# Gated MLP: the last product as a closing stage over blocks of 1024 positions, from seven products of half blocks

## Chip, cores and metric

One core of a Trainium2 chip runs the whole program. The metric is the device time of one execution in microseconds (us), median of several runs. Differences under 0.2% (2 us here) are not told from no change.

## What is computed

Three stages follow one another on a batch of 8 sequences of 576 positions: attention over 32 memory slots, a gated mixing layer, and a gated MLP. The change concerns the last one:

```python
h = np.maximum(x @ w_in, 0.0)                  # [8, 576, 1024]
u, v = h[..., :512], h[..., 512:]
v_n = (v - mean(v)) / np.sqrt(var(v) + 1e-06)  # over the last axis
v_s = np.einsum('ts,bsd->btd', w_spatial, v_n) + b_spatial[None, :, None]
gated = u * v_s                                # [8, 576, 512]
return (gated @ w_out).astype(np.float32)      # w_out: [512, 512]
```

## The kernel before

Every product of this stage is made in three terms: each fp32 operand x is split into a rounded part h (an ACT copy to the type fp32r) and the remainder x - h (a DVE subtraction); `split` (L116) makes both. `three` (L104) lists the terms h·h, l·h, h·l, and `gemm` (L94) issues the matmuls, all recorded at L99.

The MLP stage goes over eight blocks b, one for each sequence. A block has 512 positions (two halves of `HALF` = 256); the 64 positions left over of all eight sequences form a ninth block, made ahead of the loop. For each block:

- `load_x2` (L601) fetches the block's input from DRAM and forms seven operands of its quarters (four subtractions on POOL, seven splits), as steps that are called between other work.
- `uv` (L875) makes the v half of h and then the u half, each from seven products of half blocks instead of eight. A `Group` (L837) holds four output quarters; `step(q)` makes product q into a PSUM bank of its own (6 matmuls of 256 columns) and adds it to the quarters that need it: two ACT copies, five DVE additions out of PSUM and two additions on POOL or DVE for each group. Two groups alternate, in the order 1, 6, 2, 7, 5, 3, 4. When a group of v is done, `layer_norm` (L824) and `finish` (L914) normalise its tiles t and split them into `vn_h`, `vn_l` (in the buffers W3h, W3l), while PE is on the u half.
- `spatial(b, hf)` makes v_s for 288 positions at a time: for each of four chunks c, 14 matmuls of 288 columns over the tiles t = 0 to 3 of v and the left-over positions; then DVE adds the bias, multiplies by u in PSUM (L986, L995), and a split out of PSUM gives the gated values gh, gl (buffers kh, kl).
- `project(b, hf)` (L1003) makes the last product: four chunks m, each of 12 matmuls of 288 columns against the weights wo (buffers W2h, W2l), an ACT copy (L1016) and a store.

Four of a block's eight output chunks follow its spatial product; the other four are kept as `left` and called as fillers inside the next block's v and u halves, two in each. So PE's stream is: v, u (with fillers), spatial, four chunks, and so on.

The program is written in this order, but the instructions of each engine are put in their final order by a scheduler when the program is built; each engine then runs its own in that order and waits on semaphores. All DMAs of this stage are issued from SP's queue, in order.

Of the kernel before, what the change touches and what calls it, by code (L numbers as in the profile page):

```python
# [8 lines left out]
F32 = mybir.dt.float32  # L9
# [18 lines left out]
HALF = 256  # L28
# [6 lines left out]
ORDER = "ICWWKMQDWLRWqrwwaaaawaabbababxxbbwbbxxWWww"  # L35

# [7 lines left out]
def kernel(  # L44
# [40 lines left out]
    x2r = dram.tile([128, KC, B, S - 2 * HALF], F32, name="x2r", tag="x2r")  # L85
    x2d = [dram.tile([128, KC, 2 * HALF], F32, name=f"x2d{b}", tag=f"x2d{b}") for b in range(B)]
# [8 lines left out]
    def gemm(out, pairs, part=0, parts=1):  # L95

        n = len(pairs)
        for i in range(part * n // parts, (part + 1) * n // parts):
            x = nc.tensor.matmul(  # L99
                out=out, lhsT=pairs[i][0], rhs=pairs[i][1], start=i == 0, stop=i == n - 1  # L100
            )
        return x
# [422 lines left out]
    def w_in_steps():  # L525
# [61 lines left out]
        wo.extend(pair("W2", [128, KC, DM]))  # L587
        for c in range(KC):
            split(wo_raw[:, c], wo[0][:, c], wo[1][:, c])
            yield  # L590
        parts_of("W1", wi_u)
        for q, a in ((0, a11), (4, s2), (1, a12), (5, a21), (3, s1), (6, s4), (2, a22)):
            split(a, wi_u[0][:, q], wi_u[1][:, q])
            yield
# [6 lines left out]
    def load_x2(n):  # L601
# [31 lines left out]
        ts = {}  # L633
# [7 lines left out]
        if rest:  # L641
# [19 lines left out]
            yield  # L661
            put(5, b12)
            yield
            put(3, b11)
            yield
        else:
            for x in ((b12, 0, 1), (b11, 0, 0), (b21, 1, 0), (b22, 1, 1)):
                fetch_x2(*x)
            yield
            put(0, b11)  # L670
# [15 lines left out]
            yield  # L686
            put(5, b12)
            yield
            put(3, b11)
            yield  # L690
        put(6, b21)
        x2s[n] = [ts[q] for q in range(7)]
# [116 lines left out]
    def w_s_steps(places, todo):  # L809

        raw = {}
        for n, (hf, t) in enumerate(todo):
            raw[hf, t] = places[n // 3][:, n % 3 * HB:(n % 3 + 1) * HB].bitcast(F32)
            nc.sync.dma_start(out=raw[hf, t], in_=w_sT[t * 128:(t + 1) * 128, hf * HB:(hf + 1) * HB])
        yield
        for (hf, t), x in raw.items():
            ws[t, hf] = pieces.pop(0), pieces.pop(0)
            split(x, *ws[t, hf])
            yield
# [17 lines left out]
    class Group:  # L837
# [3 lines left out]
        def __init__(self, at, out, done, engine=nc.gpsimd):  # L841
            self.at, self.out, self.done, self.engine = at, out, done, engine

        def step(self, q):
            c11, c12, c21, c22 = self.out
            acc = bank(next(mm))[:, 0:HALF]
            a, b = self.at(q)
            gemm(acc, three(*a, *b))

            def add(engine, dst, x, y):  # L850
                engine.tensor_tensor(out=dst, in0=x, in1=y, op=ALU.add)  # L851

            if q == 1:
                copied[0] = nc.scalar.activation(out=c11, in_=acc, func=ACTF.Copy)
            elif q == 6:
                add(nc.vector, c12, acc, c11)
            elif q == 2:
                add(nc.vector, c11, acc, c11)
            elif q == 7:
                add(nc.vector, c21, acc, c12)  # L860
            elif q == 5:
                copied[0] = nc.scalar.activation(out=c22, in_=acc, func=ACTF.Copy)
                add(self.engine, c12, c22, c12)
                add(self.engine, c22, c22, c21)
            elif q == 3:
                add(nc.vector, c12, acc, c12)
            else:
                add(nc.vector, c21, acc, c21)
                self.done()


# [3 lines left out]
    def uv(n, fillers):  # L875
# [81 lines left out]
        def u_half(after=lambda at_: None):  # L957
            u = u_rest if rest else u_main
            products([
                Group(u_at(m), [u[:, f + m, s:s + HALF] for f in (0, 2) for s in (0, HALF)], lambda: None,  # L960
                      nc.vector if n == 0 else nc.gpsimd)
# [11 lines left out]
    gs = {}  # L973

    def spatial(b, hf):
        gh, gl = (x[:, KC * hf:KC * hf + KC, :] for x in gt)
        for c in range(KC):
# [11 lines left out]
            else:  # L989
# [9 lines left out]
            turn()  # L999
            next(x2_steps, None)  # L1000
        gs[b, hf] = (gh, gl)

    def project(b, hf):  # L1003
        gh, gl = gs.pop((b, hf))
        t0 = b * S + hf * HB

        def chunk(m):
            def do():
                ms = slice(m * 128, (m + 1) * 128)
                acc = bank(next(mm))[:, 0:HB]  # L1010
                gemm(acc, three(
                    [wo[0][:, c, ms] for c in range(KC)], [wo[1][:, c, ms] for c in range(KC)],
                    [gh[:, c, :] for c in range(KC)], [gl[:, c, :] for c in range(KC)],
                ))
                o = tile_of(next(o_tags), [128, HB])
                nc.scalar.activation(out=o, in_=acc, func=ACTF.Copy)  # L1016
                nc.sync.dma_start(out=outT[ms, t0:t0 + HB], in_=o)
                if left_v:
                    left_v.pop(0)()
                next(x2_steps, None)  # L1020

            return do

        return [chunk(m) for m in range(KC)]
# [13 lines left out]
    block = uv(0, iter(()))  # L1038
# [10 lines left out]
    pieces += [big[:, 0:HB], big[:, HB:]] + [t[:, 3584:3584 + HB] for t in wi_tiles]  # L1049
# [11 lines left out]
    rest = uv(B, iter(()))  # L1061
# [6 lines left out]
    rest.u(lambda at_: rest.late.pop(0)() if at_ == 3 else None)  # L1068
    run(more[0])
    left_v += rest.late  # L1070
    left = []
    for b in range(B):
        if b:
            block = uv(b, iter(left))
            block.v()
            block.u()
        x2_steps = load_x2(b + 1) if b < B - 1 else iter(())
        gt = pair("k", [128, FC, HB])
        spatial(b, 0)
# [68 lines left out]
```

## Time and profile before

| | us |
|---|---|
| median of 3 runs | 1010.98 (1010.49 to 1011.62) |
| span of the profiled execution | 1013.0 |
| PE busy | 989.3 (98%) |
| PEld busy | 964.3 (95%) |
| DVE busy | 681.0 (67%) |
| ACT busy | 608.5 (60%) |
| POOL busy | 113.5 (11%) |

The profile gives no other time of that execution than its span. PE is the matmul engine, PEld its weight loads, DVE the vector, ACT the scalar and POOL the general engine; SP only issues DMAs. A line number like L99 is that of the kernel file; where a helper records an operation, the names of the tiles (out<-in) tell which one it is.

### The profile page before, as it was taken

What the parts mean: (1) busy time and instruction counts of PE and PEld (TensorE: products, weight loads), DVE (VectorE), ACT (ScalarE), POOL (GpSimd) and SP (SyncE); (2) the same over time, 40 slices, a digit from 0 to 9 for tenths busy, and PEclk for the clock granted to TensorE, in tenths of its full rate; (3) what the DMA queues carried; (4) which work ended last, traced back from release to release, by engine and by line L of the source; (5) the groups of instructions that cost most, each with busy time, mean ns of one, the idle gap of its engine ahead of it and who ended that gap; (6) DMA issues with size and microseconds to landing.
All of it is one profiled execution on the core that took longest, in us unless ns stands there. A gap on an engine that the chain in (4) does not pass through costs nothing.

```text
span 1013.0 us, 20477 instructions
## 1 busy us (share of the span) xinstructions
PE 989.3 (98%) x8192; PEld 964.3 (95%) x8192; DVE 681.0 (67%) x1525; ACT 608.5 (60%) x1277; POOL 113.5 (11%) x124
## 2 busy tenths in 40 slices
PE   5889999999999999999999999999999999999998
PEld 4778999999999999999999999999999999999998
DVE  4999965675576567556667577986575757575763
ACT  4797885676678668657756475655354444445352
POOL 0000000000000000000022021412231313122220
PEclk9999999999999999999999999999999999999999
DMA  9686532233223322330042311202111111121101
GB/s 267 164 276 237 148 100 71 80 114 109 65 85 106 121 78 64 114 109 24 6 149 66 107 45 36 89 30 60 36 56 36 54 36 60 37 65 57 40 25 47
DMA packets 65135, 87.83 MB, mean 87 GB/s; under 512 B 8848, under 2 KB 57360, under 8 KB 62992
## 3 DMA queue, kind: packets, MB, share of 16 engines
q1 hardware_dynamic: 65040, 86.53, 27.6%
q8 instruction: 64, 1.05, 0.4%
q14 instruction: 31, 0.25, 0.1%
HBM read 67.77 MB, written 18.74 MB: 85 GB/s over the span
## 4 chain that ended last, share of the span: by engine, by line
PE 80%; ACT 8%; DVE 7%; DMA 3%; issue 1%; SPq 0%; POOL 0%; ACTq 0%; POOLq 0%; DVEq 0%
PE bank L99 77%; PE bank L271 2%; DMA st<-in_w_in 1%; DMA ATh<-in_kv 1%; DVE xs L118 1%; ACT t L712 1%; ACT kh L117 1%; ACT xs L117 1%; ACT t L710 1%; PE bank L323 1%; ACT xT L382 1%; DMA st<-x2d 0%; DVE kl L118 0%; ACT st L145 0%; ACT x32a L416 0%
## 5 line engine op out<-in xcount | busy, mean ns | idle before, releaser
L99 PE MATMUL bank<-xs,W1h 128*128 128x288 f32 (+1 forms) x1496 | 244.5, 292 | 1.8 <-DVE o L749 1.2
L99 PEld LDWEIGHTS bank<-xs,W1h 128*128 128x128 f32 x1496 | 210.4, 188 | 6.9 <-issue 5.8
L99 PE MATMUL bank<-xs,W1l 128*128 128x288 f32 (+1 forms) x748 | 135.5, 290 | 0.0
L99 PEld LDWEIGHTS bank<-xs,W1l 128*128 128x128 f32 x748 | 110.7, 188 | 0.2 <-issue 0.2
L118 DVE TENSOR_TENSOR kl<-t,kh 128x576 fp32r<-128x576 f32 x64 | 49.3, 771 | 58.5 <-ACT kh L117 57.9
L99 PE MATMUL bank<-xs,W2h 128*128 128x288 f32 x512 | 83.9, 298 | 1.3 <-ACT t L710 0.6
L710 ACT ACTIVATE t<-bank 128x288 f32<-128x288 f32 x128 | 50.8, 402 | 57.0 <-PE bank L99 56.6
L99 PE MATMUL bank<-kh,W3h 128*128 128x288 f32 x512 | 80.0, 297 | 1.5 <-ACT W3h L161 1.0
L99 PE MATMUL bank<-kh,W3l 128*128 128x288 f32 x512 | 80.6, 297 | 0.0
L99 PE MATMUL bank<-kl,W3h 128*128 128x288 f32 x512 | 79.2, 296 | 0.0
L99 PEld LDWEIGHTS bank<-xs,W2h 128*128 128x128 f32 x512 | 72.7, 189 | 4.6 <-issue 2.5
L99 PEld LDWEIGHTS bank<-kh,W3h 128*128 128x128 f32 x512 | 71.4, 189 | 4.1 <-ACT W3h L161 1.9
L99 PE MATMUL bank<-ATh,xs 128*128 128x256 f32 x472 | 73.6, 278 | 0.0
L99 PEld LDWEIGHTS bank<-kh,W3l 128*128 128x128 f32 x512 | 72.0, 189 | 0.8 <-issue 0.7
L99 PEld LDWEIGHTS bank<-kl,W3h 128*128 128x128 f32 x512 | 71.9, 189 | 0.0
L851 DVE TENSOR_TENSOR st<-bank,st 128x256 f32<-128x256 f32 x70 | 29.1, 424 | 63.4 <-PE bank L99 51.2
L118 DVE TENSOR_TENSOR xs<-st,xs 128x512 fp32r<-128x512 f32 (+1 forms) x60 | 54.9, 919 | 22.3 <-ACT xs L117 22.2
L117 ACT ACTIVATE xs<-st 128x512 fp32r<-128x512 f32 (+1 forms) x60 | 36.2, 624 | 49.9 <-POOL st L631 34.9
L99 PEld LDWEIGHTS bank<-ATh,xs 128*128 128x128 f32 x472 | 63.5, 188 | 0.0
L117 ACT ACTIVATE kh<-bank 128x288 fp32r<-128x288 f32 x64 | 26.0, 407 | 54.7 <-DVE bank L995 54.7
L1016 ACT ACTIVATE o<-bank 128x288 f32<-128x288 f32 x64 | 25.8, 403 | 42.7 <-PE bank L99 31.7
L371 POOL MEMSET xT<- 128x4 f32 x8 | 1.1, 133 | 434.2 <-DVE x32b L420 357.5
(270 smaller groups left out, 2212.6 us busy)
## 6 DMA issues: line engine op xcount, KB each, us to landing
ATh<-in_kv SPq DMA_DIRECT2D x14, 1300.0 KB, 6.1
out_T<-o SPq DMA_DIRECT2D x64, 144.0 KB, 1.7
ATl<-in_qT SPq DMA_DIRECT2D x30, 288.0 KB, 4.3
st<-x2d SPq DMA_DIRECT2D x32, 256.0 KB, 3.6
ATh<-in_phin SPq DMA_DIRECT2D x15, 320.0 KB, 3.2
x2d<-o SPq DMA_DIRECT2D x32, 144.0 KB, 2.0
st<-in_w_in SPq DMA_DIRECT2D x8, 512.0 KB, 4.2
ATh<-in_phiT SPq DMA_DIRECT2D x14, 288.0 KB, 2.9
```

The source lines that it names most:

```text
L99: x = nc.tensor.matmul(out=out, lhsT=pairs[i][0], rhs=pairs[i][1], start=i == 0, stop=i == n - 1)
L117: high = nc.scalar.activation(out=h, in_=x, func=ACTF.Copy)
L118: nc.vector.tensor_tensor(out=lo, in0=x, in1=h.bitcast(F32), op=ALU.subtract)
L271: x = nc.tensor.matmul(out=kvp[32 * j:32 * j + 32, :], lhsT=ph[0:n, t, 32 * j:32 * j + 32], rhs=kv[0:n, t, j, :], start=(t == 0), stop=(t ...
L323: x = nc.tensor.matmul(out=scs[hf][32 * j:32 * j + 32, :], lhsT=kmT[64 * hf:64 * hf + 64, 32 * j:32 * j + 32], rhs=q[64 * hf:64 * hf + 64, ...
L371: nc.gpsimd.memset(xT[b][:, :, 0:1], 0.0)
L382: nc.scalar.activation(out=xT[b][:, 2 * g + pr, 1 + hf * HB:1 + (hf + 1) * HB], in_=xo, func=ACTF.Copy)
L710: nc.scalar.activation(out=ks[:, m % 2 * HB:(m % 2 + 1) * HB], in_=acc, func=ACTF.Relu)
L712: nc.scalar.activation(out=ks, in_=ks, func=ACTF.Square)
L851: engine.tensor_tensor(out=dst, in0=x, in1=y, op=ALU.add)
L1016: nc.scalar.activation(out=o, in_=acc, func=ACTF.Copy)
```

## The change

All output chunks leave the block loop. `spatial` now writes the gated values as fp32 into one of two small buffers o0, o1 and stores them in DRAM (gd). After the last block a closing stage takes them in five blocks of positions (four of 1024, one of 512) and makes the product with w_out from seven products of half blocks. For this w_out is formed into seven operands once (four are kept in W2, three raw ones go to DRAM and are split in block 1).

`Group.step` is changed for all its users: the order is 1, 2, 6, 5, 7, 3, 4, and products that belong to the same running sum accumulate in one PSUM bank (x for products 1, 6, 7, 4; y for 5, 3), so that a group has four ACT copies, three DVE additions and nothing on POOL. A later product into x or y has to wait until the copy or addition that reads the bank is done.

For a closing block, `load_g` fetches four quarters, `split_g` forms seven operands of 1024 columns (nine operations on DVE and seven copies on ACT, two subtractions on POOL) and `project` runs the two groups. The forming for the next closing block is called step by step between the products; the forming for the first one is called in the spatial product of block 7, and its operands take the places of u's weights (W1), of u's inputs (xs) and of v's weights (AT).

```diff
+WIDTHS = [1024, 1024, 1024, 1024, 512]
...
         def step(self, q):
             c11, c12, c21, c22 = self.out
-            acc = bank(next(mm))[:, 0:HALF]
+            if q in (1, 2, 5):
+                self.acc = bank(next(mm))[:, 0:self.width]
+                if q == 1:
+                    self.x = self.acc
+                elif q == 5:
+                    self.y = self.acc
+            acc = self.acc if q == 2 else self.y if q in (5, 3) else self.x
             a, b = self.at(q)
-            gemm(acc, three(*a, *b))
...
+            gemm(acc, three(*a, *b), fresh=q in (1, 2, 5))
+            if q in (1, 6, 5, 4):
+                copied[0] = nc.scalar.activation(out={1: c11, 6: c12, 5: c22, 4: c21}[q], in_=acc, func=ACTF.Copy)
             else:
-                add(nc.vector, c21, acc, c21)
-                self.done()
+                dst = {2: c11, 7: c22, 3: c12}[q]
+                nc.vector.tensor_tensor(out=dst, in0=acc, in1=dst, op=ALU.add)
+            self.done(q)
+    ORDER_Q = (1, 2, 6, 5, 7, 3, 4)
...
+            g = tile_of(next(o_tags), [128, HB])
             for sl, u in parts:
                 nc.vector.scalar_tensor_tensor(
-                    out=acc[:, sl], in0=u, scalar=0.0, in1=acc[:, sl], op0=ALU.max, op1=ALU.mult
+                    out=g[:, sl], in0=u, scalar=0.0, in1=acc[:, sl], op0=ALU.max, op1=ALU.mult
                 )
-            split(acc, gh[:, c, :], gl[:, c, :])
...
+                nc.sync.dma_start(out=gd[k][:, c, p0 - 1024 * k:p1 - 1024 * k], in_=g[:, p0 - at:p1 - at])
...
+    def split_g(i):
+        w = WIDTHS[i] // 2
+        b11, b12, b21, b22 = (rows(raws[i % 2, n], w) for n in range(4))
+        t2 = rows(raws["t2"], w)
...
+        put(0, b11)
+        minus(b11, b12, b11)
+        yield
+        put(1, b21)
+        minus(t2, b22, b11)
+        yield
+        put(4, t2)
+        minus(b12, b22, b12, nc.gpsimd)
+        minus(b21, b21, t2, nc.gpsimd)
+        yield
+        put(3, b11)
+        yield
+        put(5, b12)
+        yield
+        put(2, b22)
+        yield
+        put(6, b21)
...
+        groups = [group(m) for m in range(2)]
+        for n, q in enumerate(ORDER_Q):
+            for g in groups:
+                g.step(q)
+            next(steps if n else left, None)
+            if n == 3 and i + 2 < len(WIDTHS):
+                load_g(i + 2, (0, 2, 1, 3))
...
+            block.u(lambda at_: load_g(0, (0, 2, 1, 3)) if b == B - 1 and at_ == 0 else None)
+            run(more[0])
+        if b < B - 1:
+            steps = x2_steps = load_x2(b + 1)
+        else:
...
+            steps = split_g(0)
+        spatial(b, 0, steps)
+        if b == B - 1:
+            load_g(1, (0, 2, 1, 3))
+        spatial(b, 1, steps)
+    for i in range(len(WIDTHS)):
+        left, steps = steps, split_g(i + 1) if i + 1 < len(WIDTHS) else iter(())
+        project(i, left, steps)
```

(`put` splits a value into the place of operand q; `left` in the last loop is the rest of the forming of the block itself.)

Three places show what the scheduler makes of it. The first is PE at the start of an ordinary block's spatial product. The tiles asp, t, r, xs hold the spatial weights (t those of tile t = 3 of v), W3h and W3l the split v; each bank is one chunk of the output. Before (here of block 7, the others begin alike):

```order
L99 MATMUL bank_12310<-asp,W3h 128x288 [waits DVE_49]
L99 MATMUL bank_12310<-asp,W3h 128x288 [waits Activation_49]
L99 MATMUL bank_12310<-asp,W3h 128x288
L99 MATMUL bank_12310<-t_7601,W3h 128x288 [waits Activation_49]
L99 MATMUL bank_12310<-asp,W3l 128x288
```

In the changed program, block 3:

```order
L104 MATMUL bank_9412<-asp,W3h 128x288
L104 MATMUL bank_9412<-asp,W3h 128x288 [waits Activation_49]
L104 MATMUL bank_9412<-asp,W3h 128x288
L104 MATMUL bank_9437<-asp,W3h 128x288 x3
L104 MATMUL bank_9456<-asp,W3h 128x288 [waits Activation_49]
L104 MATMUL bank_9456<-asp,W3h 128x288 x2
L104 MATMUL bank_9479<-asp,W3h 128x288 [waits Activation_49]
L104 MATMUL bank_9479<-asp,W3h 128x288 x2
L104 MATMUL bank_9502<-r,W3h 128x288 x2
L104 MATMUL bank_9502<-xs_7606,W3h 128x288
L104 MATMUL bank_9527<-r,W3h 128x288
L104 MATMUL bank_9412<-t_7602,W3h 128x288 [waits Activation_49]
```

The first matmul on tile t = 3 came fourth; now 16 matmuls on the tiles 0 to 2, of six banks, stand ahead of it.

The second place is the same in block 7 of the changed program, from the seventh matmul of the spatial product on (the six before it are on t = 0):

```order
L104 MATMUL bank_11275<-asp,W3h 128x288 [waits Activation_49]
L104 MATMUL bank_11299<-asp,W3h 128x288 [waits Activation_49]
L104 MATMUL bank_11229<-asp,W3h 128x288 [waits Activation_49]
L104 MATMUL bank_11229<-asp,W3h 128x288
L104 MATMUL bank_11252<-asp,W3h 128x288 x2
L104 MATMUL bank_11275<-asp,W3h 128x288 x2
L104 MATMUL bank_11299<-asp,W3h 128x288 x2
...
L104 MATMUL bank_11229<-t_7602,W3h 128x288 [waits Activation_49]
```

Eight matmuls on t = 0 come first, then 15 on the tiles 1 and 2 (seven of them in the rows left out), then t = 3.

The third is ACT in block 7, u half. L835 (now L858) scales a tile of v, L831 (L854) is the square root ahead of it, L117 (L123) the copy of a split; xT is an output of u. Before:

```order
L831 ACTIVATE sd<-mv,eps 128x1
L835 ACTIVATE st_11959<-st_11959,nb,sd 128x512
L117 ACTIVATE W3h<-st_11959 128x512
L831 ACTIVATE sd<-mv,eps 128x1
L1016 ACTIVATE o_12221<-bank_12208 128x288
L835 ACTIVATE st_11958<-st_11958,nb,sd 128x512
L862 ACTIVATE xT_7610<-bank_12240 128x256
L117 ACTIVATE W3h<-st_11958 128x512
```

In the changed program:

```order
L123 ACTIVATE W1h<-ATh 128x1024
L858 ACTIVATE st_10952<-st_10952,nb,sd 128x512
L123 ACTIVATE W1h<-ATh 128x1024
L123 ACTIVATE W3h<-st_10952 128x512
L854 ACTIVATE sd<-mv,eps 128x1
L879 ACTIVATE xT_7611<-bank_11113 128x256
L879 ACTIVATE xT_7611<-bank_11121 128x256
L123 ACTIVATE xs_11221<-ATh 128x1024
L123 ACTIVATE ATl<-ATh 128x1024
L123 ACTIVATE W1h<-xs_11224 128x1024
L858 ACTIVATE st_10951<-st_10951,nb,sd 128x512
L123 ACTIVATE ATl<-ATh 128x1024
```

All seven copies of 1024 columns that form the first closing block now stand between the scaling of v's first tile and the W3h copies of its last two; on DVE their seven subtractions and two differences stand in the same stretch.

## Rows read from the trace of the kernel before

**Rows 1.** stages of block 2: us, span, PE, PEld, DVE, ACT, POOL busy, clock, DMA
```profile
733.49:746.56 13.07, 13.07 (x110) 13.07 (x109) 9.72 (x29) 9.42 (x20) 3.24 (x4) 1.00 0.16 52
746.56:761.34 14.78, 14.78 (x115) 14.78 (x113) 11.99 (x25) 5.62 (x11) 6.02 (x4) 1.00 0.20 58
761.34:767.70 6.36, 6.36 (x50) 6.36 (x49) 4.44 (x14) 2.65 (x7) 0.00 (x0) 1.00 0.13 46
```

**Rows 2.** longest wait of PE from 480 us to the end: total, times, longest
```profile
PE bank L99 <- ACT kh L117: 1.1, 1, 1.1
```

**Rows 3.** PE in order of time, block 2: start us, us, instruction, tiles, count
```profile
728.48 0.62 PE L99 MATMUL bank<-ATh,xs 128*128 128x256 f32 x4
...
729.16 0.62 PE L99 MATMUL bank<-ATh,xs 128*128 128x256 f32 x4
...
730.52 0.70 PE L99 MATMUL bank<-kh,W2h 128*128 128x288 f32 x4
...
732.12 0.62 PE L99 MATMUL bank<-ATh,xs 128*128 128x256 f32 x4
...
734.67 0.64 PE L99 MATMUL bank<-xs,W1h 128*128 128x256 f32 x4
...
735.38 0.63 PE L99 MATMUL bank<-xs,W1h 128*128 128x256 f32 x4
...
746.56 0.56 PE L99 MATMUL bank<-asp,W3h 128*128 128x288 f32 x3
```

**Rows 4.** ACT in order of time, u half of block 2
```profile
736.17 0.82 ACT L835 ACTIVATE st<-st,nb,sd 128x512 f32<-128x512 f32 x1 [0.54 <-DVE nb L834]
...
738.93 0.82 ACT L835 ACTIVATE st<-st,nb,sd 128x512 f32<-128x512 f32 x1 [1.09 <-DVE nb L834]
...
741.69 0.82 ACT L835 ACTIVATE st<-st,nb,sd 128x512 f32<-128x512 f32 x1 [0.79 <-DVE nb L834]
...
744.69 0.82 ACT L835 ACTIVATE st<-st,nb,sd 128x512 f32<-128x512 f32 x1 [0.94 <-DVE nb L834]
745.54 0.63 ACT L117 ACTIVATE W3h<-st 128x512 fp32r<-128x512 f32 x1
```

**Rows 5.** DVE in order of time, same stretch
```profile
737.69 0.69 DVE L118 TENSOR_TENSOR W3l<-st,W3h 128x512 fp32r<-128x512 f32 x1
...
738.70 0.20 DVE L834 TENSOR_SCALAR nb<-mv,sd 128x1 f32<-128x1 f32 x1
```

**Rows 6.** instructions by form, 715 to 970 us: busy us, mean ns
```profile
L851 DVE TENSOR_TENSOR st<-bank,st 128x256 f32<-128x256 f32 x60 | 25.4, 425 | 59.1 <-PE bank L99 48.4 <-POOL st L851 5.7 <-ACT st L854 5.1
...
L631 POOL TENSOR_TENSOR st<-st,st 128x512 f32<-128x512 f32 x10 | 13.5, 1347 | 16.2 <-DVE xs L118 13.6 <-DMA st<-x2d 2.6
...
L862 ACT ACTIVATE st<-bank 128x256 f32<-128x256 f32 x12 | 4.6, 384 | 11.3 <-PE bank L99 11.3
```

**Rows 7.** DVE and POOL in order of time, block 2
```profile
755.38 1.33 DVE L118 TENSOR_TENSOR xs<-st,xs 128x512 fp32r<-128x512 f32 x1
...
754.87 1.29 POOL L631 TENSOR_TENSOR st<-st,st 128x512 f32<-128x512 f32 x1 [1.66 <-DVE xs L118]
```

**Rows 8.** DMA issues of the page: count, KB each, us to landing
```profile
st<-x2d SPq DMA_DIRECT2D x32, 256.0 KB, 3.6
...
st<-in_w_in SPq DMA_DIRECT2D x8, 512.0 KB, 4.2
```

**Rows 9.** start of the span: a wait of PE, and stages (1.00 is full clock)
```profile
13.55 2.55 PE L271 MATMUL bank<-ATh 128*32 128x130 f32 x40 [3.63 <-DMA ATh<-in_kv]
...
10.00:15.00 5.00, 1.45 (x28) 1.48 (x32) 1.98 (x3) 1.71 (x3) 0.00 (x0) 0.84 1.06 208
15.00:20.00 5.00, 4.87 (x50) 3.35 (x43) 2.57 (x9) 0.69 (x2) 0.00 (x0) 0.82 1.05 375
```

**Rows 10.** DVE and SP around the first spatial product
```profile
660.28 0.47 DVE L986 TENSOR_TENSOR bank<-bank,t 128x288 f32<-128x288 f32 x1
...
646.80 1.93 SPq L618 DMA_DIRECT2D st<-x2d  x4
```

More of the change, by code (lines that the diff above doesn't have):

```diff
@@ L93, in operand, with gemm @@
         return tile_of(f"xs{n}", [128, 2 * HB if n == 7 else 4 * HALF], F32R)
-    def gemm(out, pairs, part=0, parts=1):
+    def gemm(out, pairs, part=0, parts=1, fresh=True):
         n = len(pairs)
@@ L99, in gemm @@
             x = nc.tensor.matmul(
-                out=out, lhsT=pairs[i][0], rhs=pairs[i][1], start=i == 0, stop=i == n - 1
+                out=out, lhsT=pairs[i][0], rhs=pairs[i][1], start=fresh and i == 0, stop=i == n - 1,
+                skip_group_check=not fresh,
             )
@@ L686, in load_x2 @@
             yield
+            put(3, b11)
+            yield
             put(5, b12)
             yield
-            put(3, b11)
-            yield
         put(6, b21)
-        x2s[n] = [ts[q] for q in range(7)]
     def halves(tag):
@@ L816, in w_s_steps @@
         for (hf, t), x in raw.items():
+            while not pieces:
+                yield
             ws[t, hf] = pieces.pop(0), pieces.pop(0)
@@ L971, in uv, with spatial @@
         return SimpleNamespace(v=v_half, u=u_half, late=late, splits=splits)
-    gs = {}
-    def spatial(b, hf):
-        gh, gl = (x[:, KC * hf:KC * hf + KC, :] for x in gt)
+    def spatial(b, hf, steps):
         for c in range(KC):
@@ new lines, in spatial, with late_w_out @@
+            at, end = b * S + hf * HB, b * S + (hf + 1) * HB
+            p0 = at
+            while p0 < end:
+                k = p0 // 1024
+                p1 = min(end, 1024 * (k + 1))
+                nc.sync.dma_start(out=gd[k][:, c, p0 - 1024 * k:p1 - 1024 * k], in_=g[:, p0 - at:p1 - at])
+                p0 = p1
+            if left_v and c == 1:
+                left_v.pop(0)()
+            next(steps, None)
+    def late_w_out():
+        wo.extend(t[:, 0:6 * HALF].rearrange("p (n c f) -> p n c f", n=3, c=2) for t in k_tiles)
+        raw = wo[3].bitcast(F32)
+        nc.sync.dma_start(out=raw, in_=wod)
+        for _ in range(8):
+            yield
+        for n in range(3):
+            split(raw[:, n], wo[2][:, n], wo[3][:, n])
+            yield
@@ new lines, in project, with group, at, done @@
+    def project(i, left, steps):
+        w = WIDTHS[i] // 2
+        room = tile_of(("W3h", "W3l")[i % 2], [128, 4096]).rearrange("p (m k s) -> p m k s", m=2, k=4)
+        ts = gts[i]
+        def group(m):
+            ms = slice(128 * m, 128 * m + 128)
+            out = [room[:, m, k, 0:w] for k in range(4)]
+            def at(q):
+                n, x = PARTS[q]
+                h, l = (wo[0:2], wo[2:4])[n in (3, 5, 6)]
+                n = {0: 0, 1: 1, 2: 2, 4: 3, 3: 0, 5: 1, 6: 2}[n]
+                return (
+                    tuple([part[:, n, c, ms] for c in range(2)] for part in (h, l)),
+                    tuple([part[:, c, :] for c in range(2)] for part in ts[x]),
+                )
+            def done(q):
+                k = {2: 0, 3: 1, 4: 2, 7: 3}.get(q)
+                if k is not None:
+                    f, p = m + 2 * (k // 2), 1024 * i + w * (k % 2)
+                    nc.sync.dma_start(out=outT[128 * f:128 * f + 128, p:p + w], in_=out[k])
+            return Group(at, out, done, w)
+        groups = [group(m) for m in range(2)]
[5 more added lines that the diff above has]
+                load_g(i + 2, (0, 2, 1, 3))
@@ L1037 @@
         turn()
-    block = uv(0, iter(()))
+    block = uv(0)
     block.v()
@@ L1060 @@
     run(more[0])
[L1061 removed]
+    rest = uv(B)
     more[0] = chain(block.splits(), w_s_steps([operand(n) for n in (2, 6)], which[:6]))
```

137 lines of the change are left out of this document (66 added, 71 removed).

## The prediction

> **What bounds the kernel now.** I read the stages of one block first, then what PE waited for, then PE's and ACT's own order of time. In block 2 PE is busy for the whole of every stage: 13.07 us of 13.07 in the u half with its two fillers, 14.78 in the spatial product, 6.36 in four output chunks, while DVE has 9.72, 11.99 and 4.44 us of work [rows 1]. From 480 us to the end no wait of PE is longer than 1.1 us, and that one came once, ahead of the first output chunk [rows 2]. So the MLP stage is bound by PE, and a matmul removed is time removed, as long as no other engine becomes late. Two numbers show how near that is. In block 2 the last tile of v is ready as W3h at 745.54 + 0.63 = 746.17 [rows 4]; PE starts the spatial product at 746.56 [rows 3] and asks for that tile fourth. The normalisation is hidden by 0.4 us only, and two fillers are part of what hides it.
>
> **What the change removes.** Four chunks take 6.36 us [rows 1], a filler 732.12 - 730.52 = 1.60 [rows 3]. All 64 chunks go: 64 x 1.59 = **-101.8 us**.
>
> **What it adds on PE.** Four closing blocks have 7 products x 2 groups x 6 = 84 matmuls of 512 columns each, 336 in all, and the short one 84 of 256. The 256-column matmul of u comes every (735.38 - 734.67)/6 = 118 ns, that of v every (729.16 - 728.48)/6 = 113, the 288-column one every 1.60/12 = 133 [rows 3]. At the full clock of 2.4 GHz the columns alone are 106.7 and 120 ns, so 7 to 13 ns come on top. No row has 512 columns. With the same addition it is 213 + 7 to 13 = 220 to 227 ns; if time goes with columns it is 133 x 512/288 = 237. I take 224, near the constant addition, because u's and the chunk's additions (11 and 13) differ little. 336 x 0.224 + 84 x 0.118 = **+85.2 us**, between 83.8 and 89.5. The Trainium skill (TensorE: Matmul & The Clock Gate, section "Wait — 56ns, not 53.3ns?") gives a fixed 2.5 ns on top of the columns, 215.7 ns at 512; the additions of 7 to 13 ns in this trace do not agree with it; by it this term would be 82.4 and the sum 2.8 us lower.
>
> **Blocks 1 to 6: the normalisation comes into view.** Without fillers the u half lasts 13.07 - 2 x 1.60 = 9.87 us. The chain over v's four tiles goes from ACT's scaling by way of W3h, DVE's subtraction W3l, reciprocal and nb [rows 5] back to ACT; its scalings start at 736.17, 738.93, 741.69, 744.69 [rows 4], 2.8 to 3.0 us apart, and the last W3h ends 746.17 - 733.49 = 12.7 us after v. The fillers' ACT copies lie in gaps of that chain, so it doesn't shorten without them. The added u copies on ACT (0.384 each [rows 6]) fall into the same gaps, and POOL no longer disturbs it. But the scheduler has put 16 matmuls ahead of the first on tile 3: 16 x 0.132 = 2.1 us (14.78/112 is 0.132). PE asks for tile 3 at about 9.87 + 2.1 + 0.1 = 12.1, has it at 12.6, and then waits some 0.15 for its W3l: 0.65 us each, six times, **+4 us**. Bounds: nothing if the chain is half a microsecond quicker; 6 x 1.4 = 8.4 if slower by as much.
>
> **Entry into block 1.** PE now goes from the first spatial product straight into block 1, where it had 6.36 us of chunks in between. DVE is late there: it began on the first chunk at 660.28, over 9 us into the product [rows 10], and it keeps two tiles of late normalisation and gets three splits of w_out. Block 1's second pair of input loads was issued with the first from 646.80 on [rows 10]; now it waits for a buffer of the left-over block's u half and stands behind a 786 KB load of w_out. DVE's order has the operand of product 5 behind chunk 6's gating, some 17 us of DVE work after the first chunk; I put it 3 us behind PE: **+3**, between 0 and the lost cover of 6.4. The 1.1 us wait at the first output chunk [rows 2] goes: **-1.1**.
>
> **Block 7.** Here the forming of the first closing block stands inside the chain above on both engines. A 1024-column copy on ACT is 0.63 + (0.63 - 0.384) x 2 = 1.12 us (512 columns 0.63 [rows 4], 256 columns 0.384 [rows 6]); on DVE 0.69 + (0.69 - 0.425) x 2 = 1.22 ([rows 5], [rows 6]); on POOL twice 1.35 = 2.7 [rows 6]. DVE's work of the u half was 9.72 [rows 1], less four additions of 0.42: 8.0. Nine forming operations add 11.0. Two POOL subtractions run beside them; a DVE operation of 0.69 took 1.33 under POOL [rows 7], half speed, so 2.7 more. Sum 21.7, and with the hand-offs between ACT and DVE (3.3 us of idle DVE in the old half) about 25 after v's end for the last W3l, 24.2 for the last W3h. The loads (512 KB, 4.2 us to land [rows 8], four in a row) stay within that. PE has 23 matmuls, 3.0 us, before it asks for tile 3, so it waits 24.2 - 9.87 - 3.0 = 11.3, and 0.2 for W3l: **+11.5**. Bounds: 0.7, an ordinary block's wait, if the forming is no hindrance; 16 if the loads land one after the other, 4.2 each. One stretch of the wait is long, from about 13 to 20, while tile 1 is awaited. At the start of the span PE waited 3.63 us, and afterwards the granted clock was 0.84 and 0.82 over 10 us, so part of it at 1.2 GHz [rows 9]. That lost 10 x 0.17 = 1.7 us; the 15 matmuls after tile 1 have slack, so I take **+1**.
>
> **Closing stage.** DVE has for each 1024 positions 9 x 1.22 + 6 additions of 0.69 + 2.7 for POOL = 17.8 us, against PE's 84 x 0.224 = 18.8. It holds, but product 4 needs the x bank read by product 7's addition, which stands behind two subtractions under POOL: I chain it to 0.5 us late, four times, **+2**, between 0 and 8. Loads have a product order of 13 us ahead; 2 MB in and 2 MB out in 18.8 us is 220 GB/s, below the 375 moved at the start [rows 9].
>
> **Costed at nothing:** the gated stores (they replace the output stores); the two o buffers (a store has two chunks, 3.7 us, to land; 256 KB took 3.6 [rows 8]; a late one delays DVE, not PE, with eight banks); the x and y banks in u and v (a later product comes three products, 2 us, after the one that is read out, and the copy takes 0.38; where DVE is full, in the left-over block, this cover could fail, bound 2 us); forming w_out on POOL. The end is as before: a copy and a store after the last product.
>
> **Sum:** -101.8 + 85.2 + 4 + 3 - 1.1 + 11.5 + 1 + 2 = +3.8. Against the span of the profiled execution, 1013.0, that is 1016.8; this execution lies 2.0 above the median of the runs, so the median becomes **1014.8**.
>
> **Rivals.**
> (a) *Faster:* in block 7 the forming gets past in gaps of the chain, or starts so late that the W3h copies aren't behind it. Price: 11.8 less, 1003.0. It decides at the time when tile 3 is ready: below 13 us after v's end nothing is lost. Against it: seven copies stand ahead of the last two W3h in an engine that runs in order, and 21.7 us of DVE work must fit. For it: my DVE price at 1024 columns is extrapolated. Chance 0.19.
> (b) *About equal:* block 7 as worked out, but the waits of blocks 1 to 6 don't occur: 7 less, 1007.8; with half of them, 1011. Chance 0.13.
> (c) *DVE bounds the closing stage:* two POOL subtractions of 2.7 block it fully. DVE's 15.1 us without POOL become 15.1 + 5.4 = 20.5 for 1024 positions, 1.7 above PE, besides hand-offs of about 1: 4 x 2.7 - 2 = 9 more, 1024. The Trainium skill (SBUF — State Buffer, "Who interferes with whom") says that a DVE operation with two SBUF inputs against a POOL operation that reads SBUF blocks whichever started second. The half speed of [rows 7] is between that and no conflict. Chance 0.15.
> (d) *The matmuls don't shrink:* 237 ns at 512 columns, +4, is inside the range; the built program does have 768 fewer matmuls of 288 columns and 336 and 84 new ones, so that the change does nothing is left at 0.01.
>
> **Numbers.** The forecast keeps 0.52 and by itself spans 1009 to 1021. Range 1004 to 1025: it takes in (b), (c) and nearly (a). Slower by more than 0.2% (about what a measurement of this kernel can tell): most of the forecast and (c), 0.60; within 0.2%: half of (b) and the forecast's low end, 0.15; faster: (a), the rest of (b), 0.25.
>
> **What would show it.** Right: PE matmuls of 512 columns every 220 to 227 ns; PE waits on ACT's W3h at the start of each spatial product, under 1 us in blocks 2 to 6 and 9 to 13 in block 7, there with the clock below 1.00 after it; a wait on DVE xs in block 1's v half; closing blocks of about 19 us, DVE over 0.9 busy. Wrong: block 7's u half and spatial product together under 27 us, or closing blocks over 21 us.

## The result, and the profile after

The change makes the kernel slower: **1026.84 us** (median of 4 runs, 1025.05 to 1028.67) against 1011.3 for the kernel before beside it, ratio 1.0137 (95% interval 1.0106 to 1.0168). The prediction had 1014.8 and a range to 1025: the side was right, the size was not.

| profiled execution | before | after |
|---|---|---|
| span | 1013.0 | 1025.0 |
| PE busy | 989.3 | 988.3 |
| DVE busy | 681.0 | 702.0 |
| ACT busy | 608.5 | 639.4 |
| POOL busy | 113.5 | 90.5 |

PE has hardly less busy time although it has fewer columns to run. The longest waits of PE from 480 us on, which answer to [rows 2] (total, times, longest), say where to look:

```profile
PE bank L104 <- ACT W3h L123: 8.3, 7, 6.5
PE bank L104 <- ACT kh L123: 4.5, 2, 3.0
PE bank L104 <- ACT st L879: 2.7, 1, 2.7
```

There are three places, and each is followed by a low clock. Stretches of 5 us of the same execution (columns as in [rows 1]; the clock is the third number from the right):

```profile
600.00:605.00 5.00, 2.92 (x12) 2.69 (x13) 2.44 (x5) 4.94 (x11) 0.00 (x0) 0.64 0.26 76
605.00:610.00 5.00, 5.00 (x30) 5.00 (x30) 3.57 (x6) 4.77 (x10) 0.00 (x0) 0.68 0.38 130
...
675.00:680.00 5.00, 2.77 (x13) 2.78 (x14) 3.76 (x11) 1.28 (x4) 0.00 (x0) 0.65 0.20 69
680.00:685.00 5.00, 5.00 (x32) 5.00 (x32) 0.85 (x2) 1.15 (x3) 0.00 (x0) 0.67 0.00 0
685.00:690.00 5.00, 5.00 (x45) 5.00 (x44) 2.82 (x8) 3.71 (x9) 0.00 (x0) 1.00 0.01 3
...
915.00:920.00 5.00, 2.38 (x10) 2.38 (x11) 5.00 (x6) 1.76 (x3) 0.95 (x1) 0.54 0.40 123
920.00:925.00 5.00, 4.93 (x30) 4.58 (x30) 2.83 (x5) 1.44 (x2) 0.00 (x0) 0.78 0.97 338
```

PE counts as busy while its matmuls run at 1.2 GHz (5.00 of 5 us at a clock of 0.68), which is one reason why its busy time hardly fell.

**First place, ahead of the MLP: w_out's sums.** The change forms them while PE does the last V products. POOL, ACT and PE in order of time, the kernel after:

```profile
593.35 6.14 POOL L542 TENSOR_TENSOR xT<-xT 128x512 f32<-128x512 f32 x4 [0.63 <-DVE W2l L124]
...
598.17 0.63 ACT L123 ACTIVATE W2h<-xT 128x512 fp32r<-128x512 f32 x1 [5.05 <-POOL xT L542]
598.71 0.39 ACT L731 ACTIVATE t<-bank 128x288 f32<-128x288 f32 x1
599.13 0.68 ACT L733 ACTIVATE t<-t 128x576 f32<-128x576 f32 x1
599.85 0.68 ACT L123 ACTIVATE kh<-t 128x576 fp32r<-128x576 f32 x1
...
600.58 0.54 PE L104 MATMUL bank<-kh,W3h 128*128 128x288 f32 x2 [2.99 <-ACT kh L123]
602.61 2.29 PE L104 MATMUL bank<-kh,W3h 128*128 128x288 f32 x8 [1.50 <-ACT kh L123]
```

Four additions on POOL end at 599.5. The split of one sum stands in ACT's queue and waits 5.05 us for the third of them; behind it stand the copy, the square and the split of k that PE needs. From ACT's last copy of r to the first spatial product it takes 71.9 us, before it took 64.7: **7.2 us**, none of it forecast. The two ends, before and after:

```profile
586.21 0.39 ACT L728 ACTIVATE r<-bank 128x288 f32<-128x288 f32 x1
...
650.93 0.56 PE L99 MATMUL bank<-asp,W3h 128*128 128x288 f32 x3
```

```profile
584.81 0.40 ACT L749 ACTIVATE r<-bank 128x288 f32<-128x288 f32 x1
...
656.69 0.56 PE L104 MATMUL bank<-asp,W3h 128*128 128x288 f32 x3
```

**Second place, the entry into block 1.** ACT, DVE and PE, the kernel after:

```profile
674.61 0.63 ACT L123 ACTIVATE xs<-st 128x512 fp32r<-128x512 f32 x1 [3.08 <-DVE W3l L937]
676.79 0.66 ACT L879 ACTIVATE st<-bank 128x256 f32<-128x256 f32 x2 [1.55 <-DVE xs L124]
...
676.01 0.68 DVE L124 TENSOR_TENSOR xs<-st,xs 128x512 fp32r<-128x512 f32 x1
...
677.23 1.22 PE L104 MATMUL bank<-ATh,xs 128*128 128x256 f32 x4 [2.70 <-ACT st L879]
```

PE does not wait for an operand of its own, as forecast, but for ACT to read out a bank: product 6 goes into the bank x, and the copy of product 1 out of it is late because ACT waits for DVE, which still reads the buffer st. The v half lasts 15.6 us; the v half of block 2 before, with its two fillers, is the row below, and without them 12.9 - 3.2 = 9.7.

```profile
720.60:733.49 12.89, 12.89 (x111) 12.89 (x109) 3.82 (x9) 4.02 (x11) 2.90 (x4) 1.00 0.14 48
```

**Third place, block 7.** ACT, DVE and PE in the spatial stage:

```profile
912.53 1.06 ACT L123 ACTIVATE W1h<-xs 128x1024 fp32r<-128x1024 f32 x1
913.49 0.80 ACT L858 ACTIVATE st<-st,nb,sd 128x512 f32<-128x512 f32 x1
915.99 1.06 ACT L123 ACTIVATE ATl<-ATh 128x1024 fp32r<-128x1024 f32 x1 [1.70 <-POOL ATh L1054]
916.95 0.62 ACT L123 ACTIVATE W3h<-st 128x512 fp32r<-128x512 f32 x1
...
912.54 1.21 DVE L124 TENSOR_TENSOR W1l<-ATh,W1h 128x1024 fp32r<-128x1024 f32 x1
...
913.76 3.27 DVE L124 TENSOR_TENSOR W1l<-xs,W1h 128x1024 fp32r<-128x1024 f32 x1
...
917.62 2.29 PE L104 MATMUL bank<-asp,W3h 128*128 128x288 f32 x8 [6.45 <-ACT W3h L123]
...
921.66 0.61 PE L104 MATMUL bank<-t,W3h 128*128 128x288 f32 x1
```

This is the forecast picture: W3h stands behind 1024-column copies, and DVE's subtraction of 1.21 us lasts 3.27 under POOL, which subtracts from 912.63 to 915.96. The stage is 24.4 us instead of 14.8.

**Closing stage.** 88.2 us. One block in a row of the windows, and PE in order of time:

```profile
952.00:971.00 19.00, 18.98 (x84) 15.24 (x83) 16.50 (x16) 11.54 (x15) 4.81 (x2) 1.00 0.61 215
```

```profile
953.47 0.62 PE L104 MATMUL bank<-W1h,W2h 128*128 128x512 f32 x2
...
961.63 0.62 PE L104 MATMUL bank<-W1h,kh 128*128 128x512 f32 x2
...
967.18 0.64 PE L104 MATMUL bank<-ATl,kh 128*128 128x512 f32 x2
```

Between the first two rows lie 36 matmuls of 512 columns on W2's operands, 0.227 us each; between the second and the third 24 on those in kh and kl, 0.231 each. PE is full, DVE has 16.5 of 19 us.

### The profile page after: what moved, and what is told of

It is laid out like the page before. It is cut to its first block, busy times and chain, and to the rows that moved or that the text cites. A ratio compares the mean times of both kernels' runs of the same rounds, so it can differ in the third digit from the quotient of the medians.

```text
span 1025.0 us, 19854 instructions
## 1 busy us (share of the span) xinstructions
PE 988.3 (96%) x7844; PEld 944.9 (92%) x7844; DVE 702.0 (68%) x1463; ACT 639.4 (62%) x1299; POOL 90.5 (9%) x70
## 4 chain that ended last, share of the span: by engine, by line
PE 73%; DVE 11%; ACT 11%; DMA 3%; issue 2%; POOL 1%; SPq 0%; ACTq 0%; DVEq 0%; POOLq 0%
PE bank L104 70%; ACT st L858 2%; PE bank L277 2%; ACT W3h L123 1%; DVE W3l L124 1%; DMA st<-in_w_in 1%; DMA st<-in_w_v 1%; DVE st L850 1%; DVE xs L124 1%; DMA ATh<-in_kv 1%; PE bank L329 1%; ACT t L733 1%; ACT st L848 1%; ACT t L731 1%; DVE W1l L124 1%
## 5 line engine op out<-in xcount | busy, mean ns | idle before, releaser
L104 PE MATMUL bank<-kh,W3h 128*128 128x288 f32 x576 | 100.3, 299 | 6.9 <-ACT kh L123 4.5
L104 PEld LDWEIGHTS bank<-kh,W3h 128*128 128x128 f32 x576 | 84.6, 191 | 9.8 <-ACT kh L123 5.0
L104 PE MATMUL bank<-kh,W3l 128*128 128x288 f32 x544 | 90.4, 297 | 0.0
L104 PE MATMUL bank<-kl,W3h 128*128 128x288 f32 x544 | 86.1, 296 | 0.0
L104 PEld LDWEIGHTS bank<-kh,W3l 128*128 128x128 f32 x544 | 78.5, 189 | 0.8 <-issue 0.7
L104 PEld LDWEIGHTS bank<-kl,W3h 128*128 128x128 f32 x544 | 77.0, 188 | 0.0
L104 PEld LDWEIGHTS bank<-ATh,xs 128*128 128x128 f32 x472 | 67.1, 197 | 2.9 <-ACT st L879 2.9
L123 ACT ACTIVATE xs<-st 128x512 fp32r<-128x512 f32 (+1 forms) x60 | 36.4, 627 | 48.6 <-POOL st L651 24.7
L124 DVE TENSOR_TENSOR xs<-st,xs 128x512 fp32r<-128x512 f32 (+1 forms) x60 | 51.4, 864 | 10.8 <-ACT xs L123 10.5
L104 PE MATMUL bank<-ATl,xs 128*128 128x256 f32 x236 | 48.0, 286 | 0.0
L651 POOL TENSOR_TENSOR st<-st 128x512 f32<-128x512 f32 x16 | 23.2, 1452 | 272.4 <-DVE xs L124 271.7
L879 ACT ACTIVATE st<-bank 128x256 f32<-128x256 f32 x56 | 21.2, 380 | 41.5 <-PE bank L104 34.2
L733 ACT ACTIVATE t<-t 128x576 f32<-128x576 f32 x64 | 43.8, 684 | 1.2
```

The source lines that it names most:

```text
L104: x = nc.tensor.matmul(out=out, lhsT=pairs[i][0], rhs=pairs[i][1], start=fresh and i == 0, stop=i == n - 1, skip_group_check=not fresh,)
L123: high = nc.scalar.activation(out=h, in_=x, func=ACTF.Copy)
L124: nc.vector.tensor_tensor(out=lo, in0=x, in1=h.bitcast(F32), op=ALU.subtract)
L651: engine.tensor_tensor(out=out, in0=a, in1=b, op=ALU.subtract)
L733: nc.scalar.activation(out=ks, in_=ks, func=ACTF.Square)
L879: copied[0] = nc.scalar.activation(out={1: c11, 6: c12, 5: c22, 4: c21}[q], in_=acc, func=ACTF.Copy)
```

## The experiments

The theory: three pieces of preparation stand in ACT's and DVE's queues ahead of what PE needs next, and these places, with the low clock behind them, make the loss. The rival: the loss lies in the closing stage or in the clock, and a wait taken away comes back elsewhere. The measure of each place is taken from the trace, in us: *w_out* from the last copy of r to the first spatial product, *v 1* the v half of block 1, *sp 7* the spatial stage of block 7, *closing* from its end to the end of the last matmul.

| kernel | median (range) | ratio to before (95%) | w_out | v 1 | sp 7 | closing |
|---|---|---|---|---|---|---|
| before | 1011.3 | | 64.7 | | | |
| change | 1026.8 (1025.1 to 1028.7) | 1.0137 (1.0106 to 1.0168) | 71.9 | 15.6 | 24.4 | 88.2 |
| additions on DVE | 1018.9 (1017.9 to 1021.3) | 1.0076 (1.0057 to 1.0095) | 67.1 | 12.3 | 24.2 | 88.2 |
| forming held | 1022.4 (1016.8 to 1024.0) | 1.0096 (1.0066 to 1.0127) | 72.1 | 15.7 | 15.6 | 93.2 |
| splits in block 2 | 1022.9 (1021.4 to 1023.6) | 1.0109 (1.0094 to 1.0125) | 70.9 | 10.7 | 24.5 | 88.2 |
| all three | 1015.9 (1010.4 to 1019.8) | 1.0031 (1.0008 to 1.0055) | 67.1 | 10.9 | 15.6 | 92.9 |
| and closing subtractions on DVE | 1009.3 (1005.7 to 1013.9) | 0.9963 (0.9945 to 0.9982) | 68.1 | 10.8 | 15.6 | 87.1 |
| and input subtractions on DVE | **1003.7** (1003.4 to 1004.0) | **0.9909** (0.9895 to 0.9924) | 64.6 | 11.1 | 15.6 | 87.1 |

Each ratio is to runs of the kernel before that were made beside that kernel; their medians are 1011.3 for the change, 1011.8 for the next four rows and 1013.4 for the last two, so medians of different groups compare to some 2 us only.

**1. The additions of w_out on DVE.**

```diff
-        add(o22, o21, o22, ALU.add)
-        add(o21, o11, o21)
+        add(o22, o21, o22, ALU.add, nc.vector)
+        add(o21, o11, o21, engine=nc.vector)
```
(and so for the two that follow)

> The four additions that form w_out's operands go from POOL to VectorE; all else as in the change. Theory A (the POOL additions, 6.14 us in a row, hold up ACT's split of the last sum, and with it the square and split of k that stand behind it, so that PE waits 2.99 and 1.50 us and then runs some 5 us at half clock): these waits go, and the stage from the last V products to the first spatial product is some 7 us shorter; 1026.8 - 7 = 1020, and 1022 if only the waits go and the half clock stays. Rival B (the additions are only where a wait is seen; VectorE, four times 0.69 us longer in the same stage, becomes late instead): within 1 us of the change, 1026.

Measured 1018.9, 7.9 less. The w_out stretch gives 4.8 of it; 2.4 of the 7.2 stay, with one wait of 1.50 us on kh. The rest is block 1, which this edit doesn't touch: PE waited 2.38 us there instead of 2.70, and the clock did not fall behind it. PE's row and the stretch of this kernel:

```profile
673.18 0.72 PE L104 MATMUL bank<-ATh,xs 128*128 128x256 f32 x4 [2.38 <-ACT st L879]
```

```profile
675.00:680.00 5.00, 5.00 (x47) 5.00 (x46) 1.70 (x4) 2.25 (x6) 0.00 (x0) 1.00 0.07 23
```

So the POOL additions are shown as a cause, and the half clock in block 1 as a price of its own: 15.6 - 12.3 = 3.3 us, 0.3 of it the shorter wait.

**2. Forming of the first closing block held behind the last W3h of block 7.**

```diff
-            split(x, *ts[q])
+            with nullcontext() if i else tc.issue_after(normed[0].ins):
+                split(x, *ts[q])
```
(`normed[0]` is ACT's copy of the last W3h)

> In block 7 the splits of the first closing block are held behind ACT's last W3h. Theory A (seven 1024-column copies on ACT and their subtractions on VectorE stand inside the normalisation chain): the spatial stage of block 7 goes from 24.4 to about 15.1 us, the wait of 6.45 us on W3h goes, and the half clock after it; some of it may come back as VectorE is late in the first closing block, up to 3. 1026.8 - 9.3 = 1017.5, up to 1020.5. Rival B (that work bounds the stage wherever it stands: some 14 us of forming and 7.4 of gating on VectorE against 15 us of spatial product): PE waits as long at the start of the closing stage; 1024 to 1027.

Measured 1022.4, between the two cases. The spatial stage goes to 15.6 as theory A has it, 8.8 less, but the closing stage gives back 5.0, more than the 3 allowed: more than half of the gain is lost again, in the way of rival B.

**3. The late splits of w_out in block 2.** The splits are held with the same `issue_after` besides.

```diff
-            more[0] = chain(x2_steps, late_w_out()) if b == 1 else x2_steps
+            more[0] = chain(x2_steps, late_w_out()) if b == 2 else x2_steps
```

> The three late splits of w_out go from the spatial product of block 0 to that of block 2, behind ACT's last W3h there. Theory A (VectorE and ACT are full at the entry to block 1, and 3 x (0.68 + 0.63) us of this work stand ahead of the copies on which PE waits 2.70 us): block 1's v half goes from 15.6 to some 10 us, half clock included; 1026.8 - 5 = 1021.8; 1024 if a wait of about 1 us is left and with it the half clock. Rival B (the late normalisation of the left-over tiles and the gating fill VectorE there, the splits stand in gaps): no more than 1 us less, 1026.

Measured 1022.9, 3.9 less; block 1's v half is 10.7 us, the wait on the copy 0.83, the clock behind it 1.00. Theory A, with most of its size.

**4. All three.**

> The three edits together. If the three places are separate and make up the loss: 1026.8 - 7 - 9.3 - 5 = 1005.5, between 1003 and 1009, so below the kernel before (1011.3). If the loss lies in the matmuls of the closing stage (0.232 us where 0.224 was forecast) or the clock falls without those waits too: above 1015.

The profiled execution, at full clock throughout, has a span of 1008.6; but the median is 1015.9, over the upper bound of the first case and in the range of the second (above 1015). The ten runs lie between 1010.4 and 1019.8, and their mean granted clocks between 1.00 (the first) and 0.993. A clock of 0.993 over 1015 us is, by an estimate from these figures, some 7 us lost, so the half of the second case that speaks of the clock fits most of this spread. The trace that is kept is that of the first, so where the clock fell in the others stays open. What was given back is seen in the first closing block. POOL, DVE and PE:

```profile
927.16 3.37 POOL L1056 TENSOR_TENSOR xs<-xs,xs 128x1024 f32<-128x1024 f32 x1 [16.12 <-DVE st L1056]
930.49 3.37 POOL L1056 TENSOR_TENSOR st<-st,xs 128x1024 f32<-128x1024 f32 x1
...
928.24 3.37 DVE L124 TENSOR_TENSOR W1l<-st,W1h 128x1024 fp32r<-128x1024 f32 x1
931.53 0.68 DVE L882 TENSOR_TENSOR W3h<-bank,W3h 128x512 f32<-128x512 f32 x1
932.13 2.80 DVE L124 TENSOR_TENSOR W1l<-xs,W1h 128x1024 fp32r<-128x1024 f32 x1
...
932.26 0.73 PE L104 MATMUL bank<-ATl,W2h 128*128 128x512 f32 x2 [1.88 <-DVE W3h L882]
...
935.59 0.74 PE L104 MATMUL bank<-ATl,W2h 128*128 128x512 f32 x2 [1.67 <-DVE W3h L882]
```

The DVE operation that starts under POOL's ends 1.1 us after POOL's: 927.16 + 3.37 = 930.53 and 928.24 + 3.37 = 931.61, then 933.86 and 934.93. It gets nothing done while POOL runs. POOL's operation is held in its turn: a DVE subtraction (927.06 to 928.29) runs as it starts, and it takes 3.37 us, in the next closing block 2.40. The Trainium skill (SBUF — State Buffer, "Who interferes with whom") has it so: a DVE operation with two SBUF inputs and a POOL operation that reads SBUF exclude each other, and whichever starts second blocks fully; here the trace agrees, with 3.37 for 1.21. Behind it stands the addition that reads out the bank which PE's next product needs.

**5. The closing subtractions on DVE.**

```diff
-        minus(b12, b22, b12, nc.gpsimd)
-        minus(b21, b21, t2, nc.gpsimd)
+        minus(b12, b22, b12)
+        minus(b21, b21, t2)
```

> The three edits together, and the two subtractions of each closing block that stood on POOL go to VectorE. Theory A (a POOL subtraction of 1024 columns, 2.4 to 3.4 us, holds the VectorE operation beside it to its own length, 2.5 to 3.4 us instead of 1.21, so it costs VectorE 1.3 to 2.2 where the subtraction itself costs 1.21): VectorE is no longer late in the first closing block, the waits of PE there (0.79 + 1.88 + 1.67 us) shrink to under 1 in all, and the profiled span without half clock goes from 1008.6 to about 1004.5; the median from 1015.9 to 1007 to 1012, as much of it as half clock costs. Rival B (VectorE bounds the first closing block by the sum of its work, 2.4 us more of it per block): waits of 5 us or more there, span not below 1008.

Median 1009.3, span 1003.9, and no wait of PE in the closing stage: 92.9 becomes 87.1. Theory A. With two operations more DVE is earlier, since each now has its own length; the same place of the first closing block:

```profile
927.24 1.21 DVE L1056 TENSOR_TENSOR xs<-xs,xs 128x1024 f32<-128x1024 f32 x1
...
929.51 1.22 DVE L124 TENSOR_TENSOR W1l<-xs,W1h 128x1024 fp32r<-128x1024 f32 x1
```

**6. The input subtractions on DVE too** (in `load_x2`).

```diff
-            engine = nc.vector if rest else nc.gpsimd
+            engine = nc.vector
```

> As the run with the closing subtractions on VectorE, and the subtractions that form the inputs of each half block go from POOL to VectorE as well. Theory A (POOL holds VectorE in the same way ahead of the last V products and at the entry to block 1): the waits on kh (1.49 + 0.30) and on the copy st (1.02) go or halve: 1.5 to 2.5 us less than that run. Rival B (blocks 1 to 6 have VectorE at 12 of 14.8 us in the spatial stage; 4 x 0.69 us more make its operands late): waits in each of blocks 2 to 7, 0.5 each or more, so 1 to 5 us more than that run.

Median 1003.7, the best of all, 0.9% under the kernel before. The span is 1.7 under that of the run before it, and 3.2 us less pass from the last copy of r on; the wait on kh is gone, that on the copy isn't. All that PE still waits for from 590 us on (0.3 us in each of blocks 1 to 7, and once at block 1):

```profile
PE bank L104 <- ACT W3h L123: 2.2, 7, 0.3
PE bank L104 <- ACT st L879: 1.0, 1, 1.0
```

The median falls by 5.6, more than the spans: these four runs lie within 0.6 us and have clocks of 0.998 and 1.00, while the runs above still had the wait of 1.5 us on kh, and in the profile of number 5 the clock is 0.74 behind it. The clock does not explain all of that: two of the ten executions of run 5 took 1010.6 and 1013.9 at clocks of 1.00 and 0.999, and what made them long stays open. That w_out's last 2.4 us came from POOL's input subtractions follows from this run: 67.1 or 68.1 becomes 64.6. In run 5 they act in two ways: DVE's splits last longer beside them (three take 4.08 us, in this run 0.68 or 0.69 each), and ACT waits for one of them ahead of k's square:

```profile
586.81 4.08 DVE L124 TENSOR_TENSOR W2l<-xT,W2h 128x512 fp32r<-128x512 f32 x3
...
588.67 0.63 ACT L123 ACTIVATE xs<-st 128x512 fp32r<-128x512 f32 x1 [2.65 <-POOL st L651]
```

**7. The kernel before with sums in PSUM only** (the new `step` and order of products; chunks and fillers stay).

> The kernel before, with only the way in which a group of seven products is summed taken from the change (the sums in PSUM, three banks for seven products, four copies on ACT, three additions on VectorE, and the order 1, 2, 6, 5, 7, 3, 4); output chunks and fillers stay. By the prediction, which costed this part at nothing in the full blocks with a bound of 2 us in the left-over block: within 2 us of the kernel before, 1010 to 1013.5. If the sums in PSUM are themselves a part of the loss (a bank read out later holds PE): 1014 or more. If they are a hidden gain: below 1009.

1015.56 (1015.3 to 1018.6), ratio 1.0037 (1.0021 to 1.0053): some 2 to 5 us slower, not nothing. In the trace there is one wait of 1.15 us on a copy of st in block 1, and each later u half has a little more, as in this row against the 13.07 of [rows 1]:

```profile
734.90:748.30 13.40, 13.40 (x111) 13.22 (x109) 9.27 (x26) 10.81 (x24) 0.00 (x0) 1.00 0.19 60
```

The 0.3 lies in the first two products of the u half, where three matmuls start 0.06 to 0.14 us later than the others follow one another; the trace names no releaser. The u halves of the change do not have it: they take 9.9 us, as those of before do without fillers.

**8 and 9. Spare matmuls in block 7's wait.**

```diff
+        if b == B - 1:
+            out = bank(next(mm))[:, 0:128]
+            for _ in range(100):
+                nc.tensor.matmul(out=out, lhsT=ident_sb, rhs=ident_sb, start=True, stop=True)
```

> The change, with 100 spare matmuls of 128 columns, some 6 us of work, put into PE's queue ahead of block 7's spatial product, where PE waits 6.45 us for W3h; their sums are read by nobody. Theory A (PE runs at half clock for some 4.4 us after that wait because it stood still): the same end of the wait, no half clock after it, 1026.8 - 2.2 = 1024.6. Rival B (the clock falls there for another reason): 1026 to 1027.5. If the spare matmuls delay what PE has to do: above 1028.

1035.3: a miss of the experiment. The matmuls are of plain f32; one took 0.22 us, 22.5 in all, and PE was late through them. So again with 28:

> The change, with 28 spare matmuls ahead of block 7's spatial product; one took 0.225 us in the run with 100 of them, so 6.3 us, about the wait of 6.45 that PE has there. Theory A (standing still brings the half clock, which lasted from 917.6 to about 922 us in the change): the spatial stage stays bound by W3h, but its matmuls run at 0.132 us from the first one on; 24.4 us becomes 22 to 22.5 (the spare matmuls and the spatial product then lie between u's end and the closing stage), 1026.8 - 2.2 = 1024.6. Rival B (the clock falls at this place for another reason, or the W3h chain alone sets the stage's end): 1026 to 1027.5.

1024.0 (1021.2 to 1028.5). PE in order of time:

```profile
903.69 6.41 PE L1168 MATMUL bank<-ident 128*128 128x128 f32 x56
909.86 0.38 PE L104 MATMUL bank<-asp,W3h 128*128 128x288 f32 x1
912.20 1.72 PE L104 MATMUL bank<-asp,W3h 128*128 128x288 f32 x11 [1.97 <-ACT W3h L123]
...
916.25 0.40 PE L104 MATMUL bank<-t,W3h 128*128 128x288 f32 x1 [0.74 <-ACT W3h L123]
```

The 11 matmuls behind the wait take 1.72 us; in the change 8 took 2.29. So the half clock did go with the standing still. But the stage did not gain: spare matmuls and spatial product take 24.3 together, as the 24.4 before, since PE now waits for the last tile instead (22.8 us after u's start, 22.4 in the change). The clause of rival B holds: in block 7 the chain sets when PE can go on, and what the half clock adds is 0.4 us at most (from the first matmul on t to the closing stage 12.1 us in the change, 11.8 here). The 2.8 us of the median come from elsewhere, block 1 among it (12.5 instead of 15.6 in the profiled execution, after a wait of 2.37).

**10. The kernel before with the input subtractions on DVE only** (the diff of run 6).

> The kernel before, with only the subtractions that form each half block's inputs moved from POOL to VectorE: what the best version has beside the change's own parts. If the gain of the best version over the kernel before (0.9909) belongs to the closing stage: no change here, ratio 0.998 to 1.002, since PE has no wait there that these subtractions cause. If it belongs to these subtractions: 0.993 to 0.997. If VectorE becomes late in the spatial stages (12 of 14.8 us busy, and the gate's low parts to split as well): 1.002 or more.

1013.2 (1009.6 to 1016.7), ratio 1.0008 (0.9989 to 1.0028): no change. So the gain of the best version is that of the closing stage, once less stands in its way. In its trace the closing stage takes 87.1 us for the 103.7 of the chunks, 16.6 less; 8.4 of that go back to the blocks (0.8 in each spatial stage of blocks 1 to 7, 0.2 in the v halves of blocks 2 to 7, 1.4 in that of block 1), which no run here took away.

## Why the prediction was wrong

Taken against the stages of before without fillers (v 9.69, u 9.87, spatial 14.78), the profiled executions give:

| term | forecast | measured |
|---|---|---|
| chunks, fillers and first-chunk wait removed | -102.9 | -103.7 |
| closing stage, waits included | +87.2 | +88.2 |
| entry to block 1 (v half) | +3 | +5.9 |
| blocks 1 to 6, the rest | +4 | +5.9 |
| block 7 | +12.5 | +10.1 |
| w_out formed ahead of the MLP | 0 | +7.2 |
| sum | +3.8 | +13.6 |

The spans differ by 12.0, mainly since this execution reached the last copy of r 1.4 us sooner (from 10 to 20 us its granted clock was 1.00, that of before 0.84 and 0.82 [rows 9]). The medians differ by 15.5, since before's profiled execution lay 3.8 above its median (its span of 1013.0 lacks the 1.8 us that a run has around it; the prediction's "2.0 above" forgot those, which its difference doesn't feel).

- **The step that failed** is "Costed at nothing: ... forming w_out on POOL". It was priced as work of an idle engine. The cost lay in the engine that waits for it: a split of the sum stood in ACT's queue ahead of k's. Run 1 took 4.8 of the 7.2 back and run 6 the rest: beside this work even the input subtractions, which had long stood on POOL, delayed k. Without this term the time would lie inside the range (1026.8 - 7.2 = 1019.6).
- **Entry to block 1**: the place and the late DVE were right, the size was half. The forecast took the wait (3, measured 2.70) and not the clock behind it, another 3 (runs 1 and 3). It also named the wrong waiter: product 6 on the copy that empties its bank x, not product 5 on its operand. The banks x and y stood among the terms costed at nothing, with a bound of 2 us in the left-over block alone.
- **Blocks 1 to 6**: 0.65 each was forecast; the spatial stage is longer by 0.8, at the forecast place. 0.48 of it stands ahead of the first matmul on tile 3, of which 0.31 is named as the wait on W3h (the row below, block 3); most of the rest are three gaps around its W3l for which the trace names no releaser. 0.2 in each v half was missed. The upper bound of 8.4 does not follow from its half microsecond (6 x 1.15 = 6.9); nothing hung on it.

```profile
735.02 0.40 PE L104 MATMUL bank<-t,W3h 128*128 128x288 f32 x1 [0.31 <-ACT W3h L123]
```

- **Block 7**: the mechanism was right (run 2: held, the stage is 15.6), and 11.5 was 9.6. The half clock, +1 in the sum, cost 0.4 at most there (run 9). PE waited 6.45 us for W3h and not the 9 to 13 named as a sign, since at half clock it came to the last tile (921.66) just as that was ready (921.60).
- **512 columns**: 0.224 forecast, 0.227 and 0.231 measured (four products of seven and three), 336 times, so +1.6 on this term. The 215.7 ns that the Trainium skill (TensorE: Matmul & The Clock Gate, "Wait — 56ns, not 53.3ns?") gives is 11 to 15 ns below the rows, and the rows decide.
- **The x bank in the closing stage**: +2 forecast, 1.0 in the change. Rival (c) did not occur, because the first block was formed early; runs 2 and 4 made it occur in the first closing block alone (4.3 to 4.5 us), by the mechanism that was priced there. The row that the forecast read as half speed ([rows 7]) shows that mechanism already: POOL's operation ends at 754.87 + 1.29 = 756.16 and DVE's 0.55 us later, at 756.71, where its whole length is 0.69.
- **The two o buffers**, costed at nothing: in the change DVE waits nine times for their stores from 690 us on, 8.2 us in all. What of it reaches PE no run shows.
- **Sums in PSUM**, held to cost nothing in full blocks, cost the kernel before 0.37% (run 7); as the u halves of the change lack those gaps, this is no term of its sum.

## What to carry to other kernels

An operation is not free because its engine is idle: look at which queue holds its consumer, and what stands behind that one. Where two in-order engines prepare the next stage while finishing this one, hold the preparation behind the last thing that PE waits for, and then count what it leaves for the next stage. A subtraction moved to POOL to relieve DVE can cost DVE more than it saves.

## What was not expected of the hardware

- The clock behind a wait of PE, by rows of the same code in block 1: after waits of 2.70 and 2.85 us it fell (0.65 and 0.67; 0.79 and 0.53 in the two next stretches of 5 us), after 2.37 and 2.38 it stayed at 1.00. After the wait of 1.50 on kh it was 0.74 in run 5 and 1.00 in run 4. A fall cost 3 us in block 1, 1.0 between runs 4 and 5.
- A DVE subtraction of 1.21 us that starts under a POOL operation of 2.4 to 3.4 ends 1.1 us after it.
- A matmul of 128 columns in plain f32 takes 0.22 us, about as long as one of 512 columns on split operands (0.227 and 0.231).
